# Attention over packed keys with a gated convolution behind it: another order of issue

## The chip, the core and the metric

The kernel runs on one core of a Trainium2 chip. The metric is the device time of one execution in microseconds, shown as the median of 3 runs. A profile of one execution by the hardware profiler stands beside it. TensorE (PE), VectorE (DVE), ScalarE (ACT), GpSimd (POOL) and SyncE (SP, which only issues loads and stores here) each work through their own instructions in order, and semaphores tie them together.

## What is computed

Eight batches of 8 heads, 576 positions, head width 64; 32 packed queries for each head.

```python
def sm_attn(qq, kk, vv):
    s = scale * np.matmul(qq, kk.transpose(0, 1, 3, 2))
    s = s - np.max(s, axis=-1, keepdims=True)
    a = np.exp(s)
    a = a / (np.sum(a, axis=-1, keepdims=True) + 1e-09)
    return np.matmul(a, vv)
p_packed = sm_attn(p, k, v)          # 32 packed rows for each head
x = sm_attn(q, p_packed, p_packed)   # then heads side by side: 576 x 512 for each batch
gate_pre[t] = sum(conv_w[i] * x[t - 4 + i] for i in range(5))
out = (sigmoid(gate_pre) * (x @ w_val)) @ w_out
```

The weights w_val and w_out are 512 x 512. The three weights come as 64-bit floats and are turned into 32-bit ones on the chip.

## The kernel before

The work of a batch is cut into stages, and each stage is a Python generator that issues a few instructions and yields. A letter and a number name a stage: capital letters load (K, V, Q, P for a batch; L all weights), W, C and O convert w_val, the taps and w_out. Small letters compute: k and q transpose a batch's keys and queries on VectorE, a does the first attention (64 score matmuls of 32 x 32 weights, named s; row maxima nb; exponentials into a1; transposes at and their copies a1t; 48 small matmuls pv; the packed rows ppd), p turns them (ppTt, ppT), s does the second scores, t the second softmax's sums and its normalized weights a2, split into a2h and a2l. w multiplies the packed rows by w_val (wp, split into wph and wpl). x rebuilds the attention's output; for batches 0 to 2 the five taps are folded in (kx, 80 matmuls for each half), for batches 3 to 7 it is 8 + 8 matmuls and g then applies the taps on VectorE, four `scalar_tensor_tensor` rows (sig from xp and cw) for each of four channel blocks. v makes the value tiles (val, 12 matmuls with 128 x 128 weights each), multiplies them by the gate (sig from sig and val) and splits the result into gvh and gvl; o makes an output tile (12 matmuls with 512 columns, named o), copies it out (osb) and stores it.

The table ORDER, from line 50 on, is the schedule: each token such as `a2.3` advances a generator by so many yields, and `run` reads the table from left to right. `InOrder` (line 76) ties each engine's instructions together in just this order, so that nothing is reordered later: what an engine does next is the next instruction in the table's order, ready or not. A bar in the table ends the scope of the buffers in which w_val and the taps are converted (pool "stage"), and opens that of gvh and gvl. Nearly every instruction is issued through the helper, so that its line is 84.

The buffers limit how far loads run ahead: two each for a k half (km), a v piece (vm) and a q half (qm), one for p (which holds two batches), five for raw w_val tiles and taps, two for raw w_out tiles. A load waits on SP until its buffer is free, and all loads behind it wait too. PSUM has three double banks (big: scores, at, x, wp, val), one single bank for pv and ppTt (mid) and one for output tiles (out); batch 7's outputs use all of them at the end, two output tiles (4 and 5) in one double bank.

A w_val tile is converted in seven yields: two ACT rows, three VectorE rows (mask, combine, mask) and two POOL rows. Here are the combine, and the code that consumes the table:

```python
dve.scalar_tensor_tensor(
    bits, bits, 3, hw, op0=ALU.logical_shift_left, op1=ALU.bitwise_or
)
for token in order.split():
    what, n = (token + ".1").split(".")[:2]
    for _ in range(int(n)):
        next(gens[what])
```

## Time and profile before

| what | value |
|---|---|
| median of 3 runs | 290.02 us (289.56 to 290.32) |
| the profiled execution | 290.36 us, of which the span of its instructions is 288.6 us |
| PE busy | 257.3 us, 89% of the span, 3676 matmuls |
| DVE busy | 236.6 us, 82% |
| ACT busy | 163.7 us, 57% |
| POOL busy | 127.8 us, 44% |
| HBM read / written | 33.57 MB / 9.44 MB |
| o matmuls (three groups of 144) | 58.6 + 56.8 + 56.7 us of PE |
| val matmuls (three groups of 128) | 39.3 + 37.8 + 37.7 us of PE |

Busy times of matmuls overlap, since a matmul is counted until its modelled end: 12 output matmuls of about 0.4 us each take about 2.8 us together, not 4.8. In 40 slices of the span, each digit being tenths of busy time:

```profile
PE   0147758998999999999999999999999999999994
DVE  0599478598989897869999999999999899777811
DMA  6999962649576849451136456421411111111104
```

The left fifth differs from the rest: PE is not yet full there, and the DMA engines are. A row of the profile names line, engine, operation, output and inputs, shapes and count; what stands in brackets or behind the last bar is the idle time of that engine ahead of the row, and what ended it.

### The profile page before, as it was taken

Reading aid. Unit: us, or ns where it says so; the run is one execution under the profiler, and the core shown is the slowest. Engines: PE = TensorE matmul, PEld = TensorE weight load, DVE = VectorE, ACT = ScalarE, POOL = GpSimd, SP = SyncE. Lnnn points to the kernel's source line nnn. Section 1 sums busy time; section 2 is a strip of 40 time slices with the busy share of each in tenths; the row PEclk is TensorE's granted clock in tenths of the full one; section 3 lists DMA queues with packets and bytes.
Section 4 is the critical chain, followed back from the end, with each engine's and each line's share of the span. In section 5 each row is a group of like instructions: output and inputs, shape, how many; then the busy total and the mean of one; then the engine's idle time right before and its main releaser. Section 6 shows DMA issues by size and latency. Waiting matters only on the chain.

```text
span 288.6 us, 8496 instructions
## 1 busy us (share of the span) xinstructions
PE 257.3 (89%) x3676; PEld 190.6 (66%) x3676; DVE 236.6 (82%) x313; ACT 163.7 (57%) x306; POOL 127.8 (44%) x118
## 2 busy tenths in 40 slices
PE   0147758998999999999999999999999999999994
PEld 0025446476677867678678778676887688688873
DVE  0599478598989897869999999999999899777811
ACT  2363464457873646666583776566684763754322
POOL 0153668736798972305335631534044534312410
PEclk9999999999999999999999999999999999999999
DMA  6999962649576849451136456421411111111104
GB/s 238 337 354 314 297 228 75 218 131 301 185 216 201 274 111 271 154 156 41 40 125 209 140 194 204 125 75 39 118 39 39 74 39 73 40 73 73 39 0 182
DMA packets 25839, 43.56 MB, mean 151 GB/s; under 512 B 5829, under 2 KB 11973, under 8 KB 25802
## 3 DMA queue, kind: packets, MB, share of 16 engines
q1 hardware_dynamic: 25802, 43.02, 46.3%
q8 instruction: 29, 0.48, 0.7%
q14 instruction: 8, 0.07, 0.1%
HBM read 33.57 MB, written 9.44 MB: 149 GB/s over the span
## 4 chain that ended last, share of the span: by engine, by line
PE 65%; DVE 22%; ACT 5%; DMA 4%; issue 2%; POOL 0%; SPq 0%; ACTq 0%; DVEq 0%
PE o L84 27%; PE val L84 13%; DVE sig L84 10%; PE s L84 7%; PE x L84 7%; PE pv L84 4%; DMA wv_words<-in_moe_w_val_dram 4%; PE wp L84 2%; PE at L84 2%; DVE qT L84 2%; DVE t L84 2%; DVE mx L84 2%; DVE kT L84 1%; ACT sig L84 1%; DVE rs L84 1%
## 5 line engine op out<-in xcount | busy, mean ns | idle before, releaser
L84 POOL TENSOR_TENSOR gvl<-sig,gvh 128x576 fp32r<-128x576 f32 x32 | 49.0, 1533 | 85.5 <-ACT gvh L84 85.5
L84 DVE SCALAR_TENSOR_TENSOR sig<-xp,cw,sig 128x576 f32<-128x576 f32 x80 | 73.4, 917 | 6.1 <-ACT sig L84 4.5
L84 PE MATMUL o<-woh,gvh 128*128 128x512 f32 x144 | 58.6, 407 | 0.7 <-ACT osb L84 0.7
L84 PE MATMUL o<-woh,gvl 128*128 128x512 f32 x144 | 56.8, 395 | 0.0
L84 PE MATMUL o<-wol,gvh 128*128 128x512 f32 x144 | 56.7, 394 | 0.0
L84 PE MATMUL val<-a2h,wph 128*128 128x288 f32 x128 | 39.3, 307 | 0.1
L84 PE MATMUL val<-a2h,wpl 128*128 128x288 f32 x128 | 37.8, 295 | 0.0
L84 PE MATMUL val<-a2l,wph 128*128 128x288 f32 x128 | 37.7, 295 | 0.0
L84 PEld LDWEIGHTS o<-woh,gvh 128*128 128x128 f32 x144 | 27.0, 188 | 11.3 <-ACT osb L84 2.1
L84 ACT ACTIVATE osb<-o 128x512 f32<-128x512 f32 x34 | 20.2, 596 | 22.1 <-PE o L84 18.0
L84 PEld LDWEIGHTS o<-woh,gvl 128*128 128x128 f32 x144 | 27.0, 188 | 6.4
L84 ACT CAST gvh<-sig 128x576 fp32r<-128x576 f32 x32 | 21.5, 671 | 16.6 <-DVE sig L84 16.4
L84 PEld LDWEIGHTS o<-wol,gvh 128*128 128x128 f32 x144 | 27.1, 188 | 5.0
L84 PE MATMUL s<-kT,pT 32*32 32x288 f32 x512 | 17.2, 480 | 14.2 <-DVE kT L84 13.3
L84 DVE SCALAR_TENSOR_TENSOR sig<-sig,val 128x576 f32<-128x576 f32 x32 | 23.7, 740 | 7.5 <-PE val L84 4.5
L84 PEld LDWEIGHTS val<-a2h,wph 128*128 128x128 f32 x128 | 24.0, 188 | 5.7 <-issue 1.3
L84 POOL TENSOR_TENSOR t<-t,rs 128x576 f32<-128x576 f32 x16 | 20.8, 1298 | 14.7 <-DVE rs L84 14.5
L84 PEld LDWEIGHTS val<-a2h,wpl 128*128 128x128 f32 x128 | 24.1, 188 | 0.6
L84 PEld LDWEIGHTS val<-a2l,wph 128*128 128x128 f32 x128 | 24.1, 188 | 0.0
L84 PE MATMUL pv<-vm,a1t 96*32 96x64 f32 x768 | 17.0, 244 | 7.9 <-ACT a1t L84 7.3
L84 PEld LDWEIGHTS pv<-vm,a1t 96*32 96x32 f32 x768 | 13.8, 125 | 15.3 <-ACT a1t L84 9.7
L84 POOL TENSOR_TENSOR t<-t,mx 128x576 f32<-128x576 f32 x16 | 18.5, 1159 | 11.0 <-DVE mx L84 9.9
(80 smaller groups left out, 452.0 us busy)
## 6 DMA issues: line engine op xcount, KB each, us to landing
km<-in_k_dram SPq DMA_DIRECT2D x16, 576.0 KB, 5.9
vm<-in_v_dram SPq DMA_DIRECT2D x16, 576.0 KB, 5.8
qm<-in_q_dram SPq DMA_DIRECT2D x16, 576.0 KB, 6.0
out_dram<-osb SPq DMA_DIRECT2D x36, 256.0 KB, 2.0
wv_words<-in_moe_w_val_dram SPq DMA_DIRECT2D x4, 512.0 KB, 4.4
wo_words<-in_moe_w_out_dram SPq DMA_DIRECT2D x4, 512.0 KB, 5.8
p<-in_p_dram SPq DMA_DIRECT2D x16, 64.0 KB, 5.5
cw_words<-in_moe_conv_w_dram SPq DMA_DIRECT2D x1, 20.0 KB
```

What stands on the lines that cost most here:

```text
L84: made = getattr(self.engine, op)(*args, **kw)
```

## The change

Only the text of ORDER is replaced. All instructions, buffers and shapes stay; they are issued in another order, and the bar moves. The first line and the last lines of the table:

```diff
-L0 W0 L0.2 P0.2 k0 K0.2 L0 W0 L0 W0.2 L0 k0 K1 W0.2 k0 V0 W0.3 a0 O0 K1 O0 W0.2 Q0 W0.2 a0.3 V0 Q0 W0 O0 k1 W0 C0.2 O0
+L0 W0.2 P0 W0.2 L0 W0 P0 K0 k0 K0 W0.2 k0.2 W0.6 a0 L0 W0 L0 W0 K1 W0.2 a0.2 k1 a0 V0 W0.2 a0.2 K1 W0.2 L0 W0 a0 W0 a0
...
-v7 g7 v7 g7 v7 o7.2 g7 v7 o6 o7.2 v7.2 o7.15
+v7 g7.2 v7 g7.2 v7.2 o6 g7 o7 v7 o7 v7 o7.2 v7 o7.14 o6 o7 o6.2
```

What it moves, at the places that the prediction uses. First SP, the first loads of the program (wv0 to wv3 are the tiles of w_val, cw the taps, wo0 the first tile of w_out; km, vm and qm are pieces of k, v and q, with the batch and the half or group behind them). Before:

```order
L84 DMA wv0_words_77<-in_moe_w_val_dram 128x1024
L84 DMA wv1_words_81<-in_moe_w_val_dram 128x1024
L84 DMA wv2_words_83<-in_moe_w_val_dram 128x1024
L84 DMA p_0_85<-in_p_dram 32x8x64 x4
L84 DMA km_0_0_93<-in_k_dram 128x2x576
L84 DMA km_0_1_95<-in_k_dram 128x2x576
L84 DMA wv3_words_97<-in_moe_w_val_dram 128x1024
L84 DMA cw_words_100<-in_moe_conv_w_dram 5x1024
L84 DMA wo0_words_104<-in_moe_w_out_dram 128x1024
L84 DMA km_1_0_108<-in_k_dram 128x2x576
L84 DMA vm_0_0_114<-in_v_dram 96x4x384
L84 DMA km_1_1_157<-in_k_dram 128x2x576
```

And the first rows of SP now:

```order
L84 DMA wv0_words_77<-in_moe_w_val_dram 128x1024
L84 DMA p_0_82<-in_p_dram 32x8x64 x4
L84 DMA wv1_words_89<-in_moe_w_val_dram 128x1024
L84 DMA km_0_0_93<-in_k_dram 128x2x576
L84 DMA km_0_1_97<-in_k_dram 128x2x576
L84 DMA wv2_words_147<-in_moe_w_val_dram 128x1024
L84 DMA wv3_words_150<-in_moe_w_val_dram 128x1024
L84 DMA km_1_0_154<-in_k_dram 128x2x576
L84 DMA vm_0_0_166<-in_v_dram 96x4x384
L84 DMA km_1_1_174<-in_k_dram 128x2x576
L84 DMA cw_words_178<-in_moe_conv_w_dram 5x1024
L84 DMA vm_0_1_199<-in_v_dram 96x4x384
```

p and the first k halves now stand behind one and two w_val tiles instead of three, and w_out's first tile has left these rows.

Second VectorE, from its first row to the first row maximum of batch 0 (pT and kT are the transposed p and k). Before:

```order
L84 STREAM_TRANSPOSE pT_0_91<-p_0_85 128x256
L84 TENSOR_SCALAR wv0_words_77<-wv0_words_77 128x512
L84 SCALAR_TENSOR_TENSOR wv0_top_79<-wv0_top_79,wv0_words_77 128x512
L84 STREAM_TRANSPOSE kT_0_0_106<-km_0_0_93 128x1152
L84 TENSOR_SCALAR wv0_words_77<-wv0_top_79 128x512
L84 STREAM_TRANSPOSE kT_0_1_112<-km_0_1_95 128x1152
L84 TENSOR_SCALAR wv1_words_81<-wv1_words_81 128x512
L84 SCALAR_TENSOR_TENSOR wv1_top_117<-wv1_top_117,wv1_words_81 128x512
L84 TENSOR_SCALAR wv1_words_81<-wv1_top_117 128x512
L84 TENSOR_REDUCE nb1_0_0_166<-s1_0_0_121 128x1
```

The same rows of VectorE now:

```order
L84 TENSOR_SCALAR wv0_words_77<-wv0_words_77 128x512
L84 SCALAR_TENSOR_TENSOR wv0_top_79<-wv0_top_79,wv0_words_77 128x512
L84 TENSOR_SCALAR wv0_words_77<-wv0_top_79 128x512
L84 STREAM_TRANSPOSE pT_0_95<-p_0_82 128x256
L84 STREAM_TRANSPOSE kT_0_0_101<-km_0_0_93 128x1152
L84 STREAM_TRANSPOSE kT_0_1_103<-km_0_1_97 128x1152
L84 TENSOR_SCALAR wv1_words_89<-wv1_words_89 128x512
L84 SCALAR_TENSOR_TENSOR wv1_top_105<-wv1_top_105,wv1_words_89 128x512
L84 TENSOR_SCALAR wv1_words_89<-wv1_top_105 128x512
L84 TENSOR_SCALAR wv2_words_147<-wv2_words_147 128x512
L84 TENSOR_REDUCE nb1_0_0_158<-s1_0_0_113 128x1
```

The first tile of w_val now stands ahead of p's transpose, and nothing of w_val stands between the transposes of k.

Third VectorE again, from the first value tile's gating row of batch 0 to the second k transpose of batch 3, on which that batch's scores wait (t2 and mx2 are the second softmax's transposed scores and their maxima, sig with val the gating). Before:

```order
L84 SCALAR_TENSOR_TENSOR sig_0_0_592<-sig_0_0_592,val_0_0_752 128x576
L84 STREAM_TRANSPOSE kT_3_0_781<-km_3_0_589 128x1152
L84 TENSOR_SCALAR sm1_2_717<-sm1_2_717 128x2
L84 RECIPROCAL sm1_2_717<-sm1_2_717 128x2
L84 STREAM_TRANSPOSE kT_3_1_800<-km_3_1_770 128x1152
L84 STREAM_TRANSPOSE t2_1_802<-s2_1_0_805 128x18x32
L84 TENSOR_REDUCE mx2_1_803<-t2_1_802 128x18
L84 STREAM_TRANSPOSE t2_1_802<-s2_1_1_806 128x18x32
L84 TENSOR_REDUCE mx2_1_803<-t2_1_802 128x18
L84 SCALAR_TENSOR_TENSOR sig_0_1_593<-sig_0_1_593,val_0_1_875 128x576
```

This stretch of VectorE now:

```order
L84 SCALAR_TENSOR_TENSOR sig_0_0_585<-sig_0_0_585,val_0_0_748 128x576
L84 TENSOR_SCALAR sm1_2_707<-sm1_2_707 128x2
L84 RECIPROCAL sm1_2_707<-sm1_2_707 128x2
L84 STREAM_TRANSPOSE kT_3_0_836<-km_3_0_705 128x1152
L84 STREAM_TRANSPOSE t2_1_797<-s2_1_0_800 128x18x32
L84 TENSOR_REDUCE mx2_1_798<-t2_1_797 128x18
L84 STREAM_TRANSPOSE t2_1_797<-s2_1_1_801 128x18x32
L84 TENSOR_REDUCE mx2_1_798<-t2_1_797 128x18
L84 SCALAR_TENSOR_TENSOR sig_0_1_586<-sig_0_1_586,val_0_1_869 128x576
L84 TENSOR_REDUCE rs2_1_902<-t2_1_797 128x18
L84 RECIPROCAL rs2_1_902<-rs2_1_902 128x18
L84 STREAM_TRANSPOSE kT_3_1_910<-km_3_1_883 128x1152
```

The second k transpose has gone from ahead of the second softmax's rows to behind the gating row and a sum. On TensorE batch 3's first scores, which need it, have moved behind one more value tile and one more pv group.

At the end of TensorE the last output tile of batch 6 (o_6_3), which stood between the last two value tiles, now stands behind all output tiles of batch 7.

## Prediction

> **What bounds the kernel now.** I read the windows first, cut where the work changes character, then the chain that ended last, then the timeline of the start. In the windows each row is a stretch in us, its length, and busy time (and instruction count) of PE, PE's weight loads, DVE, ACT and POOL, then the granted clock, the share of the DMA engines and their GB/s.

> ```profile
> 12.90:41.75 28.85, 17.86 (x387) 10.46 (x388) 23.63 (x36) 14.41 (x31) 15.72 (x14) 1.00 0.94 300
> 57.65:126.00 68.35, 67.15 (x1374) 49.32 (x1374) 59.11 (x84) 43.53 (x93) 42.16 (x38) 1.00 0.66 202
> 126.00:184.00 58.00, 57.29 (x737) 44.32 (x729) 56.82 (x73) 37.12 (x66) 23.64 (x20) 1.00 0.45 144
> 184.00:281.00 97.00, 96.97 (x859) 74.84 (x859) 81.80 (x103) 54.80 (x93) 33.27 (x31) 1.00 0.15 54
> ```

> From 57.65 us on TensorE is a wall: idle 1.20 + 0.71 + 0.03 = 1.9 us out of 223. The instructions of the wall are the same before and after, so at most about 1.9 us can be won there. Between 126 and 184 VectorE is as full (56.82 of 58.00) and can become the bound. Everything else lies ahead of 57.65 us, where TensorE is idle for long stretches. The chain there and later (start, duration, what):

> ```profile
> 14.51 2.44 PE s L84 x47
> 22.73 1.51 PE pv L84 x48
> 24.24 0.83 PE at L84 x12
> 25.06 2.52 PE s L84 x64
> 29.98 0.58 ACT ppd L84 x2
> 30.61 0.92 PE ppTt L84 x3
> 31.54 0.49 ACT ppT L84
> 32.08 2.57 PE s L84 x63
> 46.81 0.90 PE ppTt L84 x3
> 47.72 5.00 PE x L84 x80
> 52.72 1.19 PE wp L84 x16
> 53.91 2.96 PE x L84 x80
> 56.88 0.72 ACT sig L84 x2
> 57.65 1.57 PE s L84 x59
> 68.33 1.57 PE s L84 x59
> 79.76 2.66 PE x L84 x80
> ```

> Same work, two speeds: 64 score matmuls take 2.5 us early and 1.57 us from 57.65 on; 80 x matmuls take 5.00, then 2.96, then 2.66. So TensorE runs at about half rate until some 53 us, though the window rows print 1.00; the granted clock is not a guide here, the durations are. The start of the first full-rate score group (batch 2, 57.65 us) is my milestone: the same instructions stand ahead of it on TensorE, and 55 rows ahead of its maxima on VectorE, in both orders. If the new order reaches it earlier, the wall moves with it.

> **The start, step by step.** These rows show what the first scores wait for:

> ```profile
> 2.10 2.03 SPq L84 DMA_DIRECT2D p<-in_p_dram  x4
> 3.99 0.66 ACT L84 ACTIVATE wv_top<-wv_words 128x512 f32<-128x512 f32 x1 [1.98 <-DMA wv_words<-in_moe_w_val_dram]
> 9.43 0.63 ACT L84 ACTIVATE p<-p 128x512 f32<-128x512 f32 x1 [4.78 <-DMA p<-in_p_dram]
> 13.09 1.37 DVE L84 STREAM_TRANSPOSE kT<-km 128x1152 f32<-128x1152 f32 x1
> ```

> p is issued behind three w_val tiles and lands at 9.43; VectorE has done nothing until then, because its first row waits for p. After the change one w_val tile stands ahead of p, and VectorE begins with that tile's conversion. The rate is 300/0.94 = 319 GB/s when the engines are busy. The first tile (0.52 MB, 1.64 us) is there at 3.99, so data begin at 2.35. Up to and with the second k half the old order moves 3 w_val + p + 2 k = 3.01 MB, the new one 2 w_val + p + 2 k = 2.49 MB: 2.35 + 2.49/0.319 = 10.2 us, against 11.8 (the row at 13.09 did not wait for it). The last k transpose ends at 10.2 + 1.36 = 11.6, the scores (2.46) at **14.0, before 16.97**. Durations for the rest:

> ```profile
> L84 DVE STREAM_TRANSPOSE kT<-km 128x1152 f32<-128x1152 f32 x16 | 21.6, 1358 | 0.0
> L84 DVE TENSOR_REDUCE nb<-s 128x1 f32<-128x576 f32 x16 | 11.6, 738 | 1.7 <-PE s L84 1.7
> L84 ACT ACTIVATE a<-s,nb 128x576 f32<-128x576 f32 x16 | 11.8, 740 | 5.0 <-DVE nb L84 5.0
> L84 ACT COPY a1t<-at 96x768 f32<-96x768 f32 x16 | 12.7, 793 | 8.8 <-PE at L84 8.7
> L84 DVE SCALAR_TENSOR_TENSOR wv_top<-wv_top,wv_words 128x512 uint32<-128x512 uint32 x4 | 4.4, 1102 | 0.1
> L84 DVE STREAM_TRANSPOSE t<-s 128x576 f32<-128x576 f32 x16 | 12.2, 760 | 3.6 <-PE s L84 3.6
> L84 POOL TENSOR_TENSOR t<-t,rs 128x576 f32<-128x576 f32 x16 | 20.8, 1298 | 14.7 <-DVE rs L84 14.5
> L84 POOL TENSOR_TENSOR kx<-ppd,cwb 128x640 f32<-128x640 f32 x3 | 4.7, 1552 | 0.0
> ```

> - Scores of batch 1 (before 25.0). From 14.0: two maxima and a short transpose, 1.9; the second exponential with its read-out, 0.9; two w_val steps on ACT at 0.66 each, 1.3; a1t 0.8; pv 1.51; at 0.83: 21.3. VectorE's side, from 15.9: 1.1 for the combine, about 1.5 for its four short rows, two k transposes 2.7: 21.2. **21.3.** What the old order had here and the new one has not: w_out's first tile between the maxima and the k transposes.
> - Second scores of batch 0 (before 32.08). 2.52 + 1.51 + 0.58 + 0.92 + 0.49 = 6.0 on TensorE and ACT; VectorE 2.52 + 0.74 + 2 x 1.36 = 6.0. **27.3.** The old order took 7.1.
> - x of batch 0 (before 47.7). Scores 2.57; on VectorE two transposes, two maxima and three short rows, 3.7; then subtraction about 1.2 and exponential and sum about 1.7; then POOL: two t by rs with kx and one a2l between, 1.3 + 1.55 + 1.4 + 1.3; last transpose 0.8: 27.3 + 15.5 would be 42.8, but the first t by rs starts in the shadow of the second sum (1.3 off): **41.5.**
> - Milestone (before 57.65). From 41.5: x 5.0, ppTt 0.9, x 2.96, eviction 0.72: **51.1.** The clock is taken to rise as late in the run of dense work as before.

> On SP the new order puts batch 2's k behind batch 1's first q half, which waits for a q buffer until the first q transpose, near 26: up to batch 2's second k half that is 3 q or v pieces, p and 2 k, 3.2 MB, 10 us, so the data are there near 38, and VectorE turns them after 42. Four us cover it; beyond that each is paid.

> So the start brings 57.65 - 51.1 = **6.6 us**. Its floor from these rows: if only the first two steps hold and the stages from 25.0 on take as long as before, 21.3 + 32.7 = 54.0, a gain of 3.7. Its ceiling I take 1 us higher, since I let every queue stand full (the 1102 ns of the combine hold waits for POOL).

> **After the milestone.** (a) The old order idles before the scores of batch 3 at 68.33: VectorE does both k transposes, four rows of the second attention and a gating row first. In the new order one k transpose (1.36) stands behind that gating row, and TensorE gets a value group and pv first. Of the 1.20 us idle in that window I count 0.9 as won (0 to 1.2). (b) The big products pay for small neighbours:

> ```profile
> 95.62 2.78 PE o L84 x12
> 102.28 2.99 PE o L84 x12
> ```

> An output group between value groups takes 2.78, one behind small matmuls 2.99, so each change between small and large costs about 0.1. The old order has 67 such changes, the new 71: +0.4 (0 to +0.8). Mixing by itself thus costs a little; what could pay for it is fewer waits, and there are hardly any left. (c) From the first tap of batch 3 to the last transposed weights of batch 5, 65 VectorE rows become 66: a q transpose out, a k and a short one in, +0.4. That run ends on the wait at 184.00 in the old order, so I charge all of it (0 to +2). (d) Tail: the last output group of batch 6 moves behind batch 7's.

> ```profile
> 184.00 0.71 PE x L84 x8
> 281.01 0.60 ACT osb L84
> 281.66 3.07 PE o L84 x12
> ```

> The pause at 281.0 (an eviction of a bank pair that the next product shares) is the same code and stays. The moved group needs the bank of a batch 7 group, whose eviction lies beside the last 3 matmuls. The end of batch 7's gating gets 2.8 us less cover, but its VectorE rows now stand channel by channel, tighter. I charge 0 (-0.6 to +1.0: the two pauses around 281). The 7 output stores at the end are the same.

> Sum: -6.6 - 0.9 + 0.4 + 0.4 + 0 = **-6.7 us**. The profiled execution took 290.36 (span 288.6), 0.34 over the median 290.02: 290.36 - 6.7 = 283.7, as a median **283.3**.

> [...] The two x groups at 47.72 and 53.91 show full rate 6 to 7 us after dense work began at 46.81. [...]

> **Rivals.**
> - *The clock rises sooner.* TensorE is nearly without gaps from pv on, one group ahead of x. If it is up for the last fifth of the first x (0.5 less), all of ppTt (0.5) and the second x takes 2.66, 1.3 us more is won: 282.0. Against it: the old run took longer. Chance 0.08.
> - *The start is bound by bytes.* Up to the second q half the new order moves 4 w_val, p, 4 k, 2 v, 2 q, 7.1 MB: at 300 GB/s that is 2.35 + 23.7 = 26.0 us, where VectorE wants it at 25.9. There is no slack, and a load also waits for its buffer. Then the stages from 25.0 take as long as before: gain 3.7 + 0.1, **286.2**. For it: DMA 0.94 busy. Against: in the old order VectorE, not data, set the pace. Chance 0.18.
> - *Slower: VectorE and POOL collide between 126 and 184.*

> ```profile
> 158.63 1.98 DVE L84 SCALAR_TENSOR_TENSOR sig<-xp,cw,sig 128x576 f32<-128x576 f32 x1
> 158.55 1.44 POOL L84 TENSOR_TENSOR gvl<-sig,gvh 128x576 fp32r<-128x576 f32 x1
> 161.19 0.81 DVE L84 SCALAR_TENSOR_TENSOR sig<-xp,cw,sig 128x576 f32<-128x576 f32 x1
> ```

> A tap that meets a POOL instruction takes 1.98 instead of 0.81, 1.17 more. [...] VectorE is the bound in this stretch, so each further collision is paid. Six eat the gain; nine give 290.0 - 6.7 + 10.5 = **293.8**. For it: the row order of POOL against the taps is new, with 20 POOL instructions here. Against: POOL is idle 59% of the stretch, and nothing puts more POOL work in. Chance 0.09.
> - *The order changes nothing.* The wall absorbs the early start, because loads or VectorE (59.11 of 68.35 busy) hold it back before 126: 290.0. Chance 0.06.

> **How the numbers follow.** Forecast 283.3 with 0.59. Its own range is 281.2 to 285.9: below, the ceiling (1.0), the rest of (a) (0.3), none of (c) and half of (b) (0.4 + 0.2) with (d) as charged; above, the rest of (c) (1.6) and of (d) (1.0). The range 280.5 to 287.9 takes in the early clock (282.0, with (a), (c) and (d) at their best) and the byte-bound start (286.2, with the rest of (c)), and leaves out about 0.17. Three tenths of a per cent is about what a measurement of this kernel can tell from no change. Faster: 0.59 + 0.18 + 0.08 = 0.85; same 0.06; slower 0.09.

> **What would show it.** Right: first scores near 10 us, the second scores of batch 0 near 27, the first x group near 41, the first 1.57 us score group near 51; TensorE idle below 2 us from there to the tail. Wrong: p later than 7 us on ACT (step one), waits for q or k data before a transpose (bytes), x rows still at 5 us for both halves (clock), several taps near 2 us between 120 and 177 with TensorE waiting (collisions), or a TensorE wait for gvl ahead of the last products (tail).

## The result

Over six executions each, taken in alternation, the changed kernel has a median of 292.91 us (292.21 to 295.4) and the kernel before 289.88 us (289.07 to 291.42): 1.0111 times, with a 95% interval of 1.0073 to 1.0148. It is 3.0 us slower; 6.7 us faster were forecast. The profiled execution took 292.21 us, its span is 290.4. What follows reads that execution.

The milestone came about when it was forecast. These are steps of the chain that ended last in the profile after (start, duration, what), to be read beside the same chain of before:

```profile
11.12 8.53 DMA vm<-in_v_dram
19.78 1.51 PE pv L84 x48
22.11 3.07 PE s L84 x63
25.65 1.42 issue
29.90 2.57 PE s L84 x62
43.52 3.00 PE x L84 x78
47.00 3.02 PE x L84 x80
50.81 0.76 PE s L84 x26
51.57 1.83 issue
53.40 1.15 PE s L84 x34
54.56 2.66 PE val L84 x12
```

The milestone, batch 2's first score group behind the eviction ahead of it, moved from 57.65 to 50.81, 6.84 us earlier. But 26 matmuls into that group TensorE stands for 1.83 us, and the value group behind it takes 2.66 instead of some 1.8 us. The windows of after, cut like those of before (stretch, length, busy time of PE, weight loads, DVE, ACT and POOL, granted clock, DMA share, GB/s):

```profile
50.80:126.00 75.20, 70.39 (x1381) 51.20 (x1383) 59.79 (x85) 44.01 (x93) 45.15 (x41) 0.98 0.72 203
126.00:184.00 58.00, 58.00 (x740) 45.23 (x739) 54.94 (x75) 38.68 (x70) 25.57 (x22) 1.00 0.43 129
184.00:278.00 94.00, 92.66 (x833) 70.96 (x831) 81.82 (x100) 52.26 (x89) 32.77 (x29) 1.00 0.19 65
280.00:290.00 10.00, 6.67 (x22) 4.89 (x21) 1.38 (x2) 1.79 (x3) 0.00 (x0) 0.83 0.41 157
```

TensorE, which was idle for 1.20 us in the first of these stretches before, is now idle for 4.81. The middle stretch has no idle time left. The third lost 1.34 us, and the clock fell at the very end. From the milestone to the start of the last matmul it is 226.68 us before and 235.46 after: the same instructions take **8.78 us more**, and that eats the start's 6.84.

What ended the stop in the score group? The timeline of all engines around it (start, duration, engine, operation, count, and in brackets the engine's idle time ahead and what ended it):

```profile
50.81 0.76 PE L84 MATMUL s<-kT,pT 32*32 32x288 f32 x26 [0.21 <-ACT sig L84]
51.61 0.62 ACT L84 CAST woh<-wo_top 128x512 fp32r<-128x512 f32 x1 [0.25 <-DVE wo_top L84]
51.61 0.43 DVE L84 TENSOR_SCALAR wo_words<-wo_top 128x512 uint32<-128x512 uint32 x1
52.17 1.04 POOL L84 TENSOR_TENSOR wo_words<-wo_words 128x512 f32<-128x512 f32 x1 [1.15 <-ACT sig L84]
53.40 1.15 PE L84 MATMUL s<-kT,pT 32*32 32x288 f32 x34 [1.83 <-issue]
```

Nothing that the profile names: in the trace the 34 matmuls wait for no semaphore, the keys of this batch were transposed by 48.19, and the other engines work on w_out. "issue" is time in which nothing that the profile shows was waited for. The list of DMA queues (packets, MB, share of the 16 engines' time) offers a suspect:

```profile
q8 instruction: 29, 0.48, 0.7%
```

Queue 8 moves 29 packets, all of 16,384 bytes in the trace's DMA records. TensorE runs 3676 matmuls and 3676 weight loads: 7352 / 29 = 254 to a packet. So I read the packets as TensorE's program, in blocks; no view says what is in them. How long TensorE works on 254 instructions is an estimate from rows of before: about 3.4 us in scores (59 matmuls and their weight loads in 1.57 us), but 19 us in value products (12 and theirs in 1.80).

One packet starts at 50.93, 0.6 us ahead of the stop, and in the 5.2 us before it SP had issued five loads, at 45.78, 46.24, 48.22, 48.68 and 49.15, 2.9 MB in all.

The tail is the second loss. Chain and timeline of after, end of the program:

```profile
270.50 2.07 DVE sig L84
...
278.09 0.51 PE o L84
278.63 0.60 ACT osb L84
279.28 7.41 PE o L84 x24
```

```profile
278.09 0.49 PE L84 MATMUL o<-woh,gvl 128*128 128x512 f32 x1 [0.83 <-POOL gvl L84]
279.28 0.50 PE L84 MATMUL o<-woh,gvh 128*128 128x512 f32 x1 [0.69 <-ACT osb L84]
...
281.06 0.63 PE L84 MATMUL o<-woh,gvh 128*128 128x512 f32 x1
```

TensorE waits for the last gvl, which it did not before, then for the bank as before; and from 280.3 to 283.6 its matmuls follow at 0.43 instead of 0.23 us.

### The profile page after: what moved, and what is told of

It reads as the page before. It is cut to its first block, busy times and chain, and to the rows that moved or that the text cites. A ratio compares the mean times of both kernels' runs of the same rounds, so it can differ in the third digit from the quotient of the medians.

```text
span 290.4 us, 8500 instructions
## 1 busy us (share of the span) xinstructions
PE 259.9 (89%) x3676; PEld 191.6 (66%) x3676; DVE 233.8 (81%) x313; ACT 163.8 (56%) x306; POOL 129.1 (44%) x118
## 4 chain that ended last, share of the span: by engine, by line
PE 64%; DVE 16%; ACT 7%; DMA 5%; issue 3%; POOL 2%; SPq 1%; POOLq 1%; ACTq 0%; DVEq 0%
PE o L84 25%; PE val L84 13%; DVE sig L84 11%; PE s L84 9%; PE x L84 7%; PE pv L84 4%; PE at L84 3%; DMA vm<-in_v_dram 3%; PE wp L84 2%; ACT sig L84 2%; DMA km<-in_k_dram 2%; POOL t L84 1%; PE ppTt L84 1%; SPq L84 1%; ACT gvh L84 1%
## 5 line engine op out<-in xcount | busy, mean ns | idle before, releaser
L84 POOL TENSOR_TENSOR gvl<-sig,gvh 128x576 fp32r<-128x576 f32 x32 | 49.6, 1550 | 83.5 <-ACT gvh L84 83.3
L84 DVE SCALAR_TENSOR_TENSOR sig<-xp,cw,sig 128x576 f32<-128x576 f32 x80 | 71.3, 892 | 4.5 <-ACT sig L84 3.1
L84 PE MATMUL o<-woh,gvh 128*128 128x512 f32 x144 | 59.4, 413 | 1.2 <-ACT osb L84 1.2
L84 PE MATMUL o<-woh,gvl 128*128 128x512 f32 x144 | 57.7, 401 | 0.9 <-POOL gvl L84 0.8
L84 PE MATMUL o<-wol,gvh 128*128 128x512 f32 x144 | 57.3, 398 | 0.0
L84 PE MATMUL val<-a2h,wph 128*128 128x288 f32 x128 | 39.7, 310 | 0.0
L84 ACT ACTIVATE osb<-o 128x512 f32<-128x512 f32 x34 | 20.3, 598 | 33.1 <-PE o L84 24.1
L84 PE MATMUL val<-a2h,wpl 128*128 128x288 f32 x128 | 38.2, 299 | 0.0
L84 PE MATMUL val<-a2l,wph 128*128 128x288 f32 x128 | 38.1, 298 | 0.0
L84 PEld LDWEIGHTS o<-woh,gvh 128*128 128x128 f32 x144 | 27.4, 190 | 13.9 <-ACT osb L84 3.7
L84 PEld LDWEIGHTS o<-woh,gvl 128*128 128x128 f32 x144 | 27.4, 190 | 8.1 <-POOL gvl L84 1.8
L84 PEld LDWEIGHTS o<-wol,gvh 128*128 128x128 f32 x144 | 27.5, 191 | 5.0
L84 PE MATMUL s<-kT,pT 32*32 32x288 f32 x512 | 17.7, 468 | 14.3 <-DVE kT L84 11.1
L84 DVE SCALAR_TENSOR_TENSOR sig<-sig,val 128x576 f32<-128x576 f32 x32 | 23.8, 743 | 8.1 <-PE val L84 4.2
L84 PEld LDWEIGHTS val<-a2h,wph 128*128 128x128 f32 x128 | 24.3, 190 | 5.6 <-issue 1.8
L84 ACT CAST gvh<-sig 128x576 fp32r<-128x576 f32 x32 | 21.5, 671 | 11.4 <-DVE sig L84 11.2
L84 POOL TENSOR_TENSOR t<-t,rs 128x576 f32<-128x576 f32 x16 | 20.6, 1290 | 12.7 <-DVE rs L84 9.4
L84 POOL TENSOR_TENSOR t<-t,mx 128x576 f32<-128x576 f32 x16 | 19.6, 1224 | 12.1 <-DVE sm L84 7.7
L84 DVE STREAM_TRANSPOSE kT<-km 128x1152 f32<-128x1152 f32 x16 | 21.8, 1360 | 3.8 <-DMA km<-in_k_dram 3.8
L84 PEld LDWEIGHTS val<-a2h,wpl 128*128 128x128 f32 x128 | 24.4, 190 | 0.6
L84 PEld LDWEIGHTS val<-a2l,wph 128*128 128x128 f32 x128 | 24.5, 191 | 0.0
L84 ACT ACTIVATE sig<-sig 128x576 f32<-128x576 f32 x20 | 13.7, 686 | 17.6 <-DVE sig L84 17.6
```

The costliest lines, as they stand in the source:

```text
L84: made = getattr(self.engine, op)(*args, **kw)
```

## The experiments

Theory F: a packet of TensorE's program waits behind data loads; TensorE runs dry in a run of small matmuls, where by the estimate a block is used up fastest. Rival O: that order outruns its program whatever the loads do. Rival D: VectorE's chain sets the end, and a stop of TensorE costs nothing. For the tail: less ready work ahead of the last gvl, or VectorE's chain alone.

### The loads taken away

In both orders batches 2 to 7 use batch 1's k, q and v tiles, so that 36 loads of 0.59 MB go and all other instructions stay (the attention of these batches is then computed from batch 1's data):

```diff
+        if b >= 2:
+            st[nm, b] = st[nm, 1]
+            yield
+            yield
+            return
         parts = st[nm, b] = []
```

The changed order:

> The changed order, but no k, q or v of batches 2 to 7 is loaded: batch 1's tiles are used again in their place (the attention of batches 2 to 7 is computed from batch 1's k, q and v). The engines' instructions and their order stay; 36 loads of 0.58 MB go. Theory F (TensorE stops because packets of its instructions wait behind data loads): behind the first score group of batch 2 no stop of TensorE on issue over 0.3 us, packets start within 1.5 us of the place in TensorE's program at which the fastest of them start, and the time is 4 to 7 us under the changed kernel's, 286 to 289. Rival O (TensorE's runs of small matmuls outrun the fetch even when nothing is in its way): the stops stay, time within 2 us of the changed kernel's. Rival D (VectorE's chain): the stops go, the time falls by under 2 us.

The order of before:

> The same cut in the order of before: batches 2 to 7 use batch 1's k, q and v again. Theory F: before has one stop of that kind behind its first score group of batch 2 (1.2 us at 67), so 0.5 to 2.5 us under before, 287.5 to 289.5, and the changed order with the same cut at the same time or below it. If the cut takes as much from both orders (4 us or more each), the loads cost something that is no matter of the order.

Measured: 286.6 us (286.37 to 286.92) for the changed order, 0.9887 times before (0.9839 to 0.9934), and 287.72 for the order of before, 0.9918 times (0.9888 to 0.9947). The chain of the changed order without loads, at the place of the stop:

```profile
49.51 3.06 PE x L84 x80
53.35 1.57 PE s L84 x59
54.92 1.80 PE val L84 x12
```

The score group runs through, and the value group is back at 1.80. Behind it no stop of TensorE on issue of 0.3 us is left in either kernel. Rival O falls: TensorE's order is untouched. The changed order gained 6.3 us, the order of before 2.5, at the upper edge of what F allowed. Rival D, which allowed under 2 us, falls as well: the end moved with TensorE.

### Which half of the change costs

The two orders joined at the first step of batch 2's first attention; every step not yet taken follows in the other order. Here the changed start with the rest of before, as an edit of the changed table's line 54:

```diff
-... x0 k2 O0 x0 K3 a2 t0 q1 x0 O0 v0 O0.2 V2 O0.4 a2.3 k3 a2 v0 a2.2 s1 a2
+... x0 k2 O0 x0 K3 a2 L0 V2 O0.5 t0 x0 q1 v0 O0 a2.2 K3 a2 k3 a2 v0 k3 a2.2
```

> The changed order up to the first score group of batch 2, and from there on every step in the order of before. If the loss lies in the changed order behind that place (the tail, 3 us in the profile, and the gaps at 77 and 117 us): 286 to 289.5, faster than before, with no wait for gvl ahead of the last products. If the start itself is what spoils the rest (its loads and its lead over VectorE): 290 to 293. If the whole gain of the start is kept: 283 to 285.

> The order of before up to the first score group of batch 2, and from there on every step in the changed order. If the loss lies behind that place: 292 to 296, slower than before by 2 to 6 us, with the wait for gvl of about 0.8 and a lowered clock at the end. If it lies in the start: 288 to 291.

Measured: 289.68 us for the changed start with the rest of before, 1.0008 times before (0.9973 to 1.0042); 295.05 for the start of before with the changed rest, 1.0196 times (1.013 to 1.0262). So the changed rest costs 5 us by itself. But the changed start, at its milestone 5.9 us ahead in that profile (51.79), brings nothing at the end even with the old rest: TensorE's profile there has stops on issue inside groups at 58, 77 and 83 us (1.95, 0.62 and 0.56). The same join without the loads tells whether the start is worth anything:

> The same cut of the loads in the kernel with the changed start and the order of before behind it. If the changed start is worth its 4 us wherever instructions come in time: 283 to 285, that is 3 to 5 us below the order of before with the same cut (287.7). If the lead of the start is lost later on VectorE or elsewhere for a cause other than the packets: 286.5 to 288.

It is: 284.85 us (283.89 to 286.46) against 287.72, 2.9 below the order of before with the same cut, just under the forecast.

### The tail

The changed order up to batch 7's mixing, then the order of before. The end of the table:

```diff
-v7 g7.2 v7 g7.2 v7.2 o6 g7 o7 v7 o7 v7 o7.2 v7 o7.14 o6 o7 o6.2
+g7 o6 v7 g7.3 v7 g7 v7 g7 v7 o7.2 g7 v7 o6 o7.2 v7.2 o7.15
```

> The changed order up to the first step of batch 7's mixing, the rest in the order of before. Tail theory (the last product group of batch 6 stands behind batch 7's, the gating of batch 7 goes channel by channel on VectorE, and TensorE runs out of ready work): 1.5 to 3.5 us under the changed kernel, no wait for gvl, the clock at 0.93 or more over 280 to 290. Rival D (VectorE's chain through batch 7 ends when it ends, whatever TensorE has left): the last gvl still ends at about 278, and the time is within 0.8 us of the changed kernel's.

Measured: 292.12 us (290.98 to 293.35), 1.0068 times before (1.0037 to 1.0099): some 0.8 below the changed kernel, less than the tail theory wanted, and the intervals overlap. The wait for gvl is gone. (Its profile comes to the milestone 2.2 us later than that of the changed kernel, at 53.00, and takes 1.95 us less behind it.) With the loads cut, runs scatter less, so there again:

> The changed order without the loads of k, q and v of batches 2 to 7 (batch 1's tiles used again; that kernel took 286.6), with the steps from batch 7's mixing on in the order of before. Tail theory (the changed place of batch 6's last product and the channel-by-channel gating leave TensorE without ready work ahead of the last gvl): 0.8 to 2 us less, 284.6 to 285.8, no wait for gvl. Rival D (VectorE's chain ends at the same time whatever the order): 286.2 to 287.

Measured: 284.75 us (282.89 to 285.95) against 286.6, so 1.9 less. Its chain ends like that of before, with one long run of output products and one pause:

```profile
262.45 11.22 PE o L84 x48
273.69 0.61 ACT osb L84
274.34 3.07 PE o L84 x12
```

From the milestone on it takes 226.69 us, against 227.78 with the changed tail: 1.09 us are the tail's. The rival, an end at the same time whatever the order, is out, but half of it holds: the last gvl is ready 220.5 us behind the milestone with the old tail, 220.7 with the changed one and 220.7 in the kernel before, so that VectorE's chain sets this time in either order. What differs is what TensorE still has to do then: the old tail runs 48 output products through that moment, the changed one waits 0.81 us for gvl and has batch 6's last tile left behind it.

### The loads moved

If the loads are the cause, moving them should help, with the full work. First the changed kernel with the five loads ahead of the stop held back (the write of one element of each partition makes the load wait for VectorE):

```diff
-... x0 k2 O0 x0 K3 a2 t0 q1 x0 O0 v0 O0.2 V2 O0.4 a2.3 k3 a2 v0 a2.2 s1 a2
+... x0 k2 O0 x0 a2 t0 q1 K3 x0 O0 v0 O0.2 V2 O0.4 a2.3 k3 a2 v0 a2.2 s1 a2
...
+            if (nm, b, n) == ("k", 3, 0):
+                dve.memset(m[:, 0, 0:1], 0.0)
             sp.dma_start(m, at[:, :, 2 * n : 2 * n + 2])
```

> The changed kernel, with one edit: the five loads that it issues at 45.8 to 49.2 us (two of k, two of v, one of w_out) are held back to about 49.4 by a write of one element into the first of them on VectorE, behind the transpose of q of batch 1. TensorE's order is untouched. Theory F (a 16,384-byte packet of the instruction queue, which brings TensorE's next instructions, waits behind those loads): the packet that started at 50.93 starts before 48, the gap of 1.83 in the middle of batch 2's first score group is under 0.3, the group takes under 2 us instead of 4.57, the value group behind it 1.8 instead of 2.66, and the time falls by 1 to 3.5 us. Rival O (TensorE's own run of small matmuls outruns the fetch whatever the loads do): the gap stays at 1.5 to 2 us and the time within 0.8 us of the changed kernel's. Rival D (VectorE's chain through batch 7 sets the end): the gap goes, and the time moves by under 1 us all the same.

Measured: 295.2 us, 1.0148 times before (1.007 to 1.0227), no gain. The chain, of the longest of four executions (296.45):

```profile
53.43 1.57 PE s L84 x59
55.00 1.78 PE val L84 x12
57.53 1.75 PE s L84 x57
59.51 1.65 issue
61.16 0.86 PE pv L84 x43
```

F was right about the place and wrong about the price: the stop in the score group is gone, the packet started after 1230 of TensorE's instructions instead of 1442, and the next one, at 58.54, came late in its stead; there are further stops at 83.72 (1.56 us) and 121.17 (1.58). Next, on the changed start with the rest of before, eight loads held behind TensorE's own steps:

```diff
+    GATED = [('k', 3, 1), ('v', 3, 0), ('q', 2, 0), ('k', 4, 0), ('q', 2, 1), ('v', 4, 0), ('q', 3, 0)]
+    def behind_pe(made, what):
+        if what in GATED:
+            tc.add_manual_dep(
+                made.ins,
+                pe.last,
+                mybir.DependencyInfo(mybir.DependencyClass.Sync, mybir.DependencyReason.DATA),
...
```

(The list names seven; the eighth, the other k of batch 4, stands right behind one of them.)

> The reference's full work again: the changed order up to the first score group of batch 2, the order of before behind it (the kernel that took 289.7), and its loads paced. Eight loads of k, q and v between about 48 and 90 us wait, by an edge to TensorE's step ahead of them in the order, until the packet of TensorE's instructions that is due has started; two of v and one of w_out change places with them. Theory F: the stops on issue at 58, 77 and 83 us (2.2, 1.0, 0.8) go, and the time falls by 2 to 4 us to 285.5 to 288, faster than before. Rival (data that now comes later stops the engines instead): waits on DMA of k, q or v appear on VectorE or TensorE between 55 and 90, and the time stays at 289 to 291.

Measured: 295.45 us, 1.0170 times before (1.0134 to 1.0207). The rival happened, at more than its price. VectorE's list of waits (waited for: us in total, times, longest):

```profile
DVE kT L84 <- DMA km<-in_k_dram: 7.1, 3, 3.6
DVE qT L84 <- DMA qm<-in_q_dram: 4.0, 4, 2.3
```

Behind the milestone the stops on issue went, and the data came late. That is not the whole loss, though. This profile ends 7.6 us after that of the same kernel without the pacing, and 4.1 us of it lie ahead of the milestone (55.92 against 51.79), where TensorE has a stop on issue of 3.43 us at 37.10, before the first held load; the two programs are alike up to there, so this part belongs to the scatter of the start. So the opposite: loads issued as early as their buffers allow, in the order in which these come free. One line of the table, against the kernel without pacing:

```diff
-a1 x0 K2 w0 k2 O0 a1 x0 O0 L0 x0 O0 w0 x1 p1.2 x0 k2 O0 x0 K3 a2 L0 V2 O0.5 t0 x0 q1 v0 O0 a2.2 K3 a2 k3 a2 v0 k3 a2.2
+K2 w0 k2 O0 a1 x0 O0 L0 V2 Q2 V2 K3 x0 O0 w0 x1 p1.2 x0 k2 K3 L0 O0 x0 a2 O0.5 t0 x0 q1 Q2 v0 O0 a2.3 k3 P4 L0 a2 v0
```

> The reference's full work: the changed order up to the first score group of batch 2, the order of before behind it (the kernel that took 289.7, whose stops on issue stood at 58, 77 and 83 us), with its loads spread the other way, to earlier places: 13 loads from 39 us on (v, q and k of batches 2 and 3, k of batch 4, two of w_out) are issued as soon as their buffers come free, in that order, so that 40 to 46 us, when the queue idled, is used and no six of them stand together ahead of a packet; only one of q ahead of 30 us and one ahead of 78 us are held back, behind TensorE's step ahead of them in the order. Theory F: the stops behind the score group of batch 2 fall from 4.8 us to under 2, no new wait for data, and the time is 285.5 to 288.5. Rival (any bunch only moves the stop to the next packet, as with the two kernels whose loads were held back): stops stay at 4 us or more in all, 289 to 291.

Measured: 290.19 us (287.78 to 292.25), 0.9979 times before (0.9952 to 1.0007): no difference that can be told. The stops at 58, 77 and 83 are gone, and behind the milestone one is left, longer:

```profile
52.91 0.76 PE s L84 x26
53.66 3.48 issue
57.15 2.12 PE s L84 x34
59.27 3.19 PE val L84 x12
```

Two of those loads held back behind TensorE's steps, the first k of batch 3 and the first tile of w_out:

```diff
-    GATED = [('q', 1, 0), ('q', 3, 0)]
+    GATED = [('q', 1, 0), ('q', 3, 0), ('k', 3, 0), 'wo0']
```

> The kernel with the loads spread to earlier places, and two of them held back: the first k of batch 3 (issued at 47.9 us there, 0.1 us ahead of the place at which the packet due then starts when nothing is in its way; the packet came at 54.6, TensorE stood for 3.5 us) waits for the ppTt group ahead of it in the order, and the first tile of w_out for the first pv group (the first packet started 4.6 us late there). Theory F: the packet due at 48 starts by 49.5, the stop of 3.5 us goes, no other comes in its place, and the time is 285.5 to 288, under before by 2 to 4 us. Rival (the stop only moves to the next packet): 289 to 291.

Measured: **287.86 us** (285.41 to 289.69), 0.9922 times before (0.9894 to 0.9951): faster than both kernels, with the full work. Not quite as forecast, though:

```profile
50.79 0.76 PE s L84 x26
51.55 1.74 issue
53.29 2.12 PE s L84 x34
55.41 3.19 PE val L84 x12
```

The stop is halved, not gone, and more of the gain lies ahead of the milestone (50.79 against 52.91), which moves by as much from profile to profile of one start (below). The last attempt holds three more loads at that place and puts the second v of batch 2 behind both k of batch 3:

> As the kernel before it (287.9), with more held back at the one place that still stops: there the packet due at about 46 started at 50.5, behind one q and one v of batches 2 that were issued at 41.4 and 43.4 and two k issued at 47. Here the second v of batch 2 stands behind both k of batch 3, and the third tile of w_out and both q of batch 2 wait for the first value product (about 54 us). Theory F: the packet starts by 47.5, the stop of 1.7 us in batch 2's first score group goes, and the time falls by 0.5 to 2.5 us more, to 285.5 to 287.5. Rival (the bytes are the same and the next packet, due at about 53, is late in its place): a stop of 1 to 2 us near 57 instead, 287.5 to 289.

Measured: 289.13 us, 1.0001 times before (0.996 to 1.0043). The stop in the score group went, and smaller ones came at 66 (0.94 us) and 78 (0.42). Its interval lies just above that of the order ahead of it (0.9894 to 0.9951), so it is probably the worse of the two. But in the profiles the part behind the milestone is 1.7 us shorter than there (229.74 against 231.4) and the milestone 2.2 later (53.01): the stops behind it became cheaper, and why the start is later is open.

### What the kernels show together

From the traces: the number of TensorE instructions (matmuls and weight loads) ahead of each stop on issue inside a group, of 0.4 us or more, in all kernels of the study.

| instructions ahead | found in |
|---|---|
| 443 | all but before without loads (in pv of batch 0) |
| 696 | changed; loads later; paced; the three with the changed start and no loads |
| 1456 | changed; loads earlier; loads earlier, two held |
| 1710 | loads later; changed start with the rest of before; tail of before |
| 1966 | held more |
| 2474 | changed; changed start with the rest of before; held more |
| 2727 to 2730 | loads later; both joined orders; tail of before |
| 3745 to 3747 | loads later; start of before with the changed rest |
| 3999 to 4001 | changed; loads later; start of before with the changed rest; tail of before |

The distances are 253, 3 x 253, 254, 256, 2 x 254, 254 to 256, 4 x 254 and 254. In these profiles such stops stand only at these places, in every order. Other waits do not keep to them: before stands 0.77 us for a VectorE row at 1852. The fifth packet, by this reading the one that brings what lies behind 1456:

| kernel | packet starts | instructions issued by then | stop at 1456 |
|---|---|---|---|
| before | 51.95 | 1196 | none |
| loads later | 48.75 | 1230 | none |
| held more | 48.14 | 1226 | none |
| changed, no loads | 50.24 | 1284 | none |
| loads earlier, two held | 50.48 | 1404 | 1.74 us |
| changed | 50.93 | 1442 | 1.83 us |
| loads earlier | 54.63 | 1456 | 3.48 us |

In the three kernels that stop, TensorE starts again 2.5 to 2.8 us after the start of the packet, and the stop is the longer the more instructions were issued by then (1.74, 1.83 and 3.48 us at 1404, 1442 and 1456).

The same count at the places that follow, packets 6 to 16, shows what the loads do. In the four kernels without the loads every one of these packets starts at most 1.6 us after TensorE has begun the block ahead of the one that it brings. With the loads it is up to 3.7 us later in the changed kernel, 4.2 in before and 6.0 in "held more". None starts more than 1.3 us earlier than that, in any kernel, so by this reading TensorE had little more than one block in hand. From these numbers an estimate of what a late packet may cost: a block of scores lasts 3.4 us, and 2.5 of it pass between the packet's start and its use, so in a run of scores some 0.9 us of delay is free; in value products some 16.

## Why the prediction was wrong

**The start was right in sum, by luck.** Forecast 51.1 for the milestone, measured 50.81. The steps were not: batch 1's scores began near 22.1 (forecast 21.3), the second scores of batch 0 at 29.9 (27.3), x at 43.5 (41.5). Late v data (the load of batch 0's v takes 8.5 us on the chain) and the 1.42 us stop, at instruction 443, cost those 2 us: part of the rival of a start bound by bytes. The other rival, a clock that rises sooner, gave them back, since x took 3.00 instead of 5.00: the term "x 5.0" was 2 us too large, because I had the clock rise as late as before. These steps of after show when it rose:

```profile
40.26 2.45 PE wp L84 x16
42.71 0.81 PE pv L84 x48
```

The packed rows by w_val (wp) at 40.26 still take 2.45 us, pv at 42.71 runs at full rate (0.81 instead of 1.51). The granted clock in the trace goes from half to full at 41.47, 3.5 us after TensorE began to work without a pause at 37.93. In before the record begins, at full clock, at 53.07, 6.3 us after the last pause ended at 46.81, so the time from a pause to full clock was not the same in the two. Nor is the granted clock "not a guide": the clock record of before begins only at 53.07, and the 1.00 ahead of it stands for no record; the record of after has half clock from 17.58 to 24.40 and from 27.82 to 41.47, where the products were slow.

The profile's start is a lucky one as well: eight profiles with this start have the milestone between 50.31 and 55.92, so its gain is about 2 to 7 us, and the stops at 443 and 696 move it.

**The step that failed** is the sentence "If the new order reaches it earlier, the wall moves with it." I took the work behind the milestone as fixed, because the instructions are the same. It is, where no such stop of 0.4 us or more stands behind the milestone: from the milestone to the last matmul it is 226.68 us before, 226.76 with the loads cut, 226.69 in the changed order with loads cut and the tail of before. With the loads in place the changed order takes 235.46. Of these 8.78 us, 235.46 - 227.78 = 7.7 went with the loads and 1.09 with the tail. Of the 7.7 the trace shows stops on issue of 1.83, 0.87 and 1.13 us and slower matmuls behind the first (34 score matmuls in 1.15 us, where 0.9 would do by the 1.57 for 59, and 12 value matmuls in 2.66 against 1.80, with half clock from 55.12 to 58.54), 4.9 in all; about 1.5 us is the clock's fall at 280, eight matmuls at 0.2 us more, which the kernel without loads happened not to have. Some 1.3 us stay unassigned. The trace of before had late packets too, but TensorE had large products then, whose blocks last longer by the estimate: one started at 73.58, 4.2 us after TensorE had begun the block ahead, and still 3.1 us before its instructions were due. That is read from the traces; no run tested it alone. The rival nearest to this was that the wall absorbs the early start because loads hold it back; it had loads as late data, not as late instructions, and ended at 290.0.

**The small terms** held in sum. (a) the wait ahead of batch 3's scores is gone; (b) and (c), changes between small and large groups and one more VectorE row, together with (a), come to 226.69 - 226.76 = -0.1 (kernels without loads, both with the old tail), as forecast (-0.9 + 0.4 + 0.4). Singly they are not shown: the first of these kernels also waits 1.02 us for wpl at 71.60 and 1.28 us for sig at 237.12, where the other does not, so something else paid for that. In the working, the lower end of the forecast's own range is 281.4 by the terms listed, not 281.2. The rival of VectorE and POOL colliding did not come: the middle window has no idle time. **(d) the tail** was mis-sized: I charged 0, with 1.0 as the worst, and it cost 1.1 to 1.9 us without loads, and in the changed kernel the fall of the clock besides. I had seen that the end of the gating got 2.8 us less cover and set against it that VectorE's rows stand tighter. They did not end sooner: in three of four channels a tap met POOL (1.87 to 2.07 us instead of 0.82), in the old order in one, and the last gvl was ready at 278.04, against 278.33 in before, which came to the milestone 6.84 us later.

## What to carry to other kernels

Identical instructions in another order were not identical work here: behind the milestone they took 8.78 us more, and 7.7 of that went with the loads. So where a profile lists an instruction queue, as here with 29 packets of 16,384 bytes, estimate how long the instructions of one packet last in each stretch (3.4 us in scores here, 19 in value products), and see where bursts of loads meet the short ones. In these profiles the loss showed as "issue" inside a group, at distances of about 254 instructions or a multiple of it; holding a burst of loads back by a few microseconds only moved the stop to the next such place (from 1456 to 1710, 295.2 us). Spreading them into idle time of the queue changed nothing by itself (290.19 us); with two of them held back as well it gave 287.86. And compare starts over several profiles: here the same start reached the milestone between 50.3 and 55.9 us.

## What the runs showed of the hardware

```profile
274.13 0.52 PE o L84
274.68 0.61 ACT osb L84
275.32 2.37 PE o L84 x9
```
